# Weight conversion of a fused attention and feed-forward kernel: VectorE's bit steps with PSUM operands, one ScalarE copy more per block

## The chip, the cores and the metric

The kernel runs on one core of one Trainium2 chip. The metric is the device time of one execution in microseconds (us), as the median of several runs. Engines are named as in the profile: PE (TensorE, matrix products), DVE (VectorE), ACT (ScalarE), POOL (GpSimd) and SP (SyncE, which issues the DMAs here). They run side by side, each through its own queue in order, and wait for each other by semaphores. SBUF is the working memory; PSUM is the accumulation memory that PE writes, in 8 banks of 512 float32 columns on 128 partitions. DVE and ACT can read and write PSUM, POOL can't.

## The reference

```python
def _attn_ref(q, k, v):                      # q, k, v: (8, 8, 576, 64) float32
    scores = scale * np.matmul(q, k.transpose(0, 1, 3, 2))
    kth = np.partition(scores, -top_k, axis=-1)[..., -top_k:-top_k + 1]   # top_k = 32
    scores = np.where(scores >= kth, scores, -1000000000.0)
    attn = np.exp(scores - np.max(scores, axis=-1, keepdims=True))
    attn = attn / (np.sum(attn, axis=-1, keepdims=True) + 1e-09)
    return np.matmul(attn, v).astype(np.float32)

def _moe_ref(x, w_in, conv_w, w_out):        # x: (8, 576, 512); w_in: (512, 1024); w_out: (1024, 512)
    h = np.maximum(x @ w_in, 0.0)
    conv_out = ...                           # depthwise convolution of h with conv_w, 3 taps along the sequence
    gate = 1.0 / (1.0 + np.exp(-conv_out))
    return (h * gate @ w_out).astype(np.float32)
```

The attention output, with its heads side by side, is the input `x` of the gated feed-forward part. The weights `w_in`, `conv_w` and `w_out` arrive as float64. The chip has no float64 arithmetic, so the kernel turns each number into float32 by itself, from its two 32-bit words.

## The kernel before, in words

Attention goes by tiles of 128 query rows: 32 pairs of heads with 9 tiles each, 288 tiles (`NT`). A software pipeline handles them. `iteration(it)` issues, for each engine in an order written out by hand, one stage of each of some nine neighbouring tiles, and is called once per tile. In one iteration:

- PE transposes the weighted exponentials of an older tile (`transposes`, L306), computes scores of a pair of tiles into `s_ps` (`scores`, L214 to L222, every second iteration) and multiplies by V into a corner of the same PSUM tensor (`av`, L337 and L340).
- DVE finds the 32nd largest score: seven `MAX8` over chunks of a tile (`chunk_ops`, L235) interleaved with the merging of the candidates of the tile before (`cand_ops`, L255 and L257), one `MAX8` over a whole row (`below`, L283) and `select` (L287); then `weigh` (L293) masks the exponentials, which it reads from PSUM (`e_ps`), and sums them.
- ACT makes a sign mask (`sides`, L268), copies scores out of PSUM (`evacuate`, L228), copies transposed tiles (L311) and attention outputs (L348), and computes exponentials into `e_ps` (`expo`, L280). `e_ps` is a single buffer: `expo` of the next tile can start only when `weigh` has read it.
- POOL multiplies rows by the mask (`flip`, L273), and later does parts of the feed-forward convolution.

Feed-forward work (`Expand`, `Contract`) fills the rest of PE from 212 us on, when the first batch of attention outputs is there.

The change is in the conversion of the weights. 33 blocks (`weight_blocks`: one for `conv_w`, 16 for `w_in`, 16 for `w_out`, 256 numbers per partition each but for the first) go through a pipeline of their own, one block per iteration, so that all of it lies in the first 163 us. A block passes these steps:

- `load`: SP fetches the block's raw words into `raw`, up to 12 blocks ahead.
- `split` on DVE, in iteration k: L150 masks the exponent field out of the top 16-bit word of each number, L151 masks the top of the mantissa out of the upper 32-bit word. Both write to `scratch` in SBUF.
- `act` on ACT, at the end of the same iteration, after `expo`: L155 makes the power of two out of the exponent field (an `Exp`), L156 turns the mantissa's integer into float32, L157 does so with the lower 32-bit word (`rest`).
- `sign` on DVE, in iteration k+1: L161 puts the sign bit on the power; both of its tensor inputs and its output lie in SBUF.
- `pool` on POOL, in iteration k+2: L166, L170, L171 and L172 add the two mantissa parts, multiply by the signed power and split the product into two float32 parts for PE.

Where these steps stand on DVE is set by a loop at the end of the DVE part of `iteration`: `c_first` (the two split steps) after the first two chunk maxima, `c_last` (the sign) after the whole loop, just before `weigh`.

The PSUM bank `mc` belongs to the last product of the feed-forward part (`Contract`), whose first use comes after all blocks are converted.

Of the kernel before, what the change touches and what calls it, by code (L numbers as in the profile page):

```python
# [13 lines left out]
BF16 = mybir.dt.bfloat16  # L14
U16 = mybir.dt.uint16
U32 = mybir.dt.uint32
AF = mybir.ActivationFunctionType
ALU = mybir.AluOpType
# [32 lines left out]
WB = 256  # L51
# [12 lines left out]
def attend_and_feed(ctx: ExitStack, tc: tile.TileContext, q, k, v, weights, out, shared, finish=None):  # L64
    nc = tc.nc
# [13 lines left out]
    scale = 1.0 / float(D) ** 0.5  # L79
# [26 lines left out]
    offset = const.tile([P, 1], F32, name="offset")  # L106
# [11 lines left out]
    def bank(name):  # L118
        return ps.tile([P, BANK], F32, name=name, tag=name, bufs=1)
# [4 lines left out]
    scratch = []  # L124

    class Convert:
# [5 lines left out]
        def load(self):  # L132
            i = Convert.count
            Convert.count += 1
            if not scratch:
                scratch.append(moe.tile([P, 4 * SPB, WB], F32, name="scratch", tag="split"))
            self.at = i % SPB * 4
            tag = ("x_hi", "x_lo")[i % 2]
            self.raw = xp.tile([P, self.src.shape[-1], 2], U32, name="raw64", tag=tag)[0:self.n]
            nc.sync.dma_start(out=self.raw.rearrange("a c t -> a (c t)"), in_=self.src.bitcast(U32))  # L140
# [2 lines left out]
            return scratch[0][0:self.n, self.at + i, 0:self.raw.shape[1]]  # L143

        def split(self):
            exponent, self.mantissa, self.rest = (self.tmp(i) for i in range(3))
            n = exponent.shape[1]
            self.field, self.power = exponent.bitcast(U16)[:, 0:n], exponent.bitcast(BF16)[:, n:2 * n]
            self.top = self.raw.rearrange("a c t -> a (c t)").bitcast(U16).rearrange("a (c t) -> a c t", t=4)[:, :, 3]
            yield lambda: nc.vector.tensor_scalar(self.field, self.top, 0x7FF0, None, ALU.bitwise_and)  # L150
            yield lambda: nc.vector.tensor_scalar(self.mantissa.bitcast(U32), self.raw[:, :, 1], 0xFFFFF, 0x100000,  # L151
                                                  ALU.bitwise_and, ALU.bitwise_or)

        def act(self):
            nc.scalar.activation(out=self.power, in_=self.field, func=AF.Exp, scale=math.log(2.0) / 16, bias=offset)  # L155
            nc.scalar.activation(out=self.mantissa, in_=self.mantissa.bitcast(U32), func=AF.Copy, scale=2.0 ** -20)  # L156
            nc.scalar.activation(out=self.rest, in_=self.raw[:, :, 0], func=AF.Copy, scale=2.0 ** -52)  # L157

        def sign(self):
            power = self.power.bitcast(U16)  # L160
            yield lambda: nc.vector.scalar_tensor_tensor(out=power, in0=self.top, scalar=0x8000, in1=power,  # L161
                                                         op0=ALU.bitwise_and, op1=ALU.bitwise_or)

        def pool(self):
            x = self.mantissa
# [116 lines left out]
    def below(t):  # L282
        nc.vector.max(out=t.z[:, 0:8], in_=t.z[:, 10:S + 10])  # L283

    def select(t):
        hot = att.tile([P, 10], F32, name="hot", bufs=3)
        nc.vector.scalar_tensor_tensor(out=hot, in0=above, scalar=t.cnt, in1=t.z[:, 0:10],  # L287
                                       op0=ALU.is_equal, op1=ALU.mult, accum_out=kth[:, t.n:t.n + 1])
# [404 lines left out]
    def convert_dve():  # L693
        first, last = [], []
        while acted:
            c = acted.popleft()
            last.extend(c.sign())
            dved.append(c)
        if fetched:
            c = fetched.popleft()  # L700
            first.extend(c.split())
            cut.append(c)
        return first, last
# [10 lines left out]
    def iteration(it):  # L714
        nonlocal av_next, out_next, rec_next
        n = it + 3
# [14 lines left out]
        if n < NT:  # L731
# [3 lines left out]
            t = Box()  # L735
# [23 lines left out]
        c_first, c_last = convert_dve()  # L759
        for i in range(max(7, len(a_ops), len(b_ops))):  # L760
            if i < len(a_ops):
                a_ops[i]()
            for op in c_first[i:i + 1]:
                op()
            if tD is not None and not exact:
                if i == BELOW_AT:
                    below(tD)
                if i == BELOW_AT + 2:
                    select(tD)
            if i < len(b_ops):  # L770
                b_ops[i]()
        for op in c_last:
            op()
        while gates:
            gates.popleft().gate()
        recs, rec_next = rec_next, []
# [46 lines left out]
        while pool_tasks and state.pool > 0.2 and pool_tasks[0][0] <= it:  # L823
# [3 lines left out]
            _, c, fn = pool_tasks.popleft()  # L827
# [6 lines left out]
    with tc.manual_schedule(engines=engines) if engines else nullcontext():  # L834
        for pc in pcs[0:2]:
            fetch(pc)
        load_blocks(W_FIRST)
        for it in range(-3, NT + 6):
            iteration(it)
    if finish is not None:  # L840
        finish(corner(2, 1)[0:1])
    while expands or contracts or any(x.waiting for x in lanes) or pool_tasks or tanh_next or tanh_now or gates:
        it += 1
        iteration(it)
# [121 lines left out]
```

## Time and profile before

| | |
|---|---|
| median of 3 runs | 1152.47 us (1152.42 to 1154.94) |
| the profiled execution | 1155.28 us; its span, first to last instruction, 1153.4 us |
| busy, share of the span | PE 1035.3 us (90%), DVE 1064.5 (92%), ACT 996.5 (86%), POOL 895.6 (78%) |
| chain that ended last | DVE 45%, PE 42%, ACT 11% |
| TensorE clock | mean 0.963 of full; half speed for parts of 60 to 180 us, full for nearly all of the rest |

A busy time is the sum of an engine's instructions; the durations of neighbours overlap by some 0.08 us, since a following instruction starts before the former one has ended. "Idle before" is the time an engine stood still ahead of an instruction, with what ended it. The chain that ended last is followed back from the last instruction.

### The profile page before, as it was taken

How to read it: one execution, taken by the hardware profiler on the slowest of the kernel's cores; microseconds unless marked ns; L12 is line 12 of the kernel's file. 1: busy time of each engine (PE TensorE's matmuls, PEld its weight loads, DVE VectorE, ACT ScalarE, POOL GpSimd, SP SyncE). 2: the span in 40 equal slices, each digit the busy share in tenths (PEclk: the TensorE clock that was granted, in tenths of full speed). 3: DMA queues.
4: the chain of work that ended last, by engine and by line, in shares of the span. 5: the costliest groups of instructions: out<-in, count | busy, mean ns of one | idle time of the engine just before them, and what ended most of it. 6: DMA issues, size and time to landing. Idle time of an engine off the chain costs nothing.

```text
span 1153.4 us, 27267 instructions
## 1 busy us (share of the span) xinstructions
PE 1035.3 (90%) x7970; PEld 767.3 (67%) x7970; DVE 1064.5 (92%) x5834; ACT 996.5 (86%) x2343; POOL 895.6 (78%) x1078
## 2 busy tenths in 40 slices
PE   3665676788999999999999999999999999999997
PEld 1443444566767776777777767777777677777896
DVE  7999999999999999999999999999999999998651
ACT  5777868899999999999999999999999999998442
POOL 6788864688979888898978887987978897898300
PEclk9967659999999999999999999999999999999999
DMA  7221101111111111111111112121211011110001
GB/s 242 79 68 41 46 17 40 46 38 44 55 54 56 56 46 65 46 55 56 49 38 44 56 45 64 47 64 46 64 55 56 24 38 59 55 33 21 31 28 40
DMA packets 51694, 60.75 MB, mean 53 GB/s; under 512 B 9776, under 2 KB 30544, under 8 KB 51536
## 3 DMA queue, kind: packets, MB, share of 16 engines
q1 hardware_dynamic: 51536, 58.91, 16.0%
q8 instruction: 66, 1.08, 0.4%
q14 instruction: 92, 0.75, 0.2%
HBM read 49.31 MB, written 9.58 MB: 51 GB/s over the span
## 4 chain that ended last, share of the span: by engine, by line
DVE 45%; PE 42%; ACT 11%; issue 1%; DMA 0%; SPq 0%; POOL 0%; ACTq 0%; POOLq 0%
DVE cand L235 13%; DVE e L293 9%; PE mc L554 9%; PE me L404 8%; DVE z L283 7%; PE s_ps L337 6%; PE s_ps L219 5%; PE pt L306 5%; DVE cand L257 3%; ACT weights_ps L280 2%; DVE scratch L161 2%; DVE rows L255 2%; PE s_ps L222 2%; DVE hot L287 2%; PE weights_ps L554 2%; PE s_ps L214 2%
## 5 line engine op out<-in xcount | busy, mean ns | idle before, releaser
L273 POOL TENSOR_TENSOR z<-rows,side 128x579 f32<-128x579 f32 x288 | 347.4, 1206 | 143.0 <-ACT side L268 122.5
L235 DVE MAX8 cand<-rows 128x8 f32<-128x82 f32 (+1 forms) x2016 | 451.0, 238 | 0.0
L280 ACT ACTIVATE weights_ps<-rows,z 128x576 f32<-128x576 f32 x288 | 219.8, 763 | 42.4 <-DVE e L293 31.5
L293 DVE SCALAR_TENSOR_TENSOR e<-rows,kth,weights_ps 128x576 f32<-128x576 f32 x288 | 230.1, 799 | 0.3
L268 ACT ACTIVATE side<-rows 128x576 bf16<-128x576 f32 x288 | 224.2, 778 | 0.8 <-DVE rows L255 0.5
L404 PE MATMUL me<-x_hi,wi 128*128 128x322 f32 (+1 forms) x928 | 218.6, 308 | 1.2 <-ACT g L418 1.2
L283 DVE MAX8 z<-z 128x8 f32<-128x576 f32 x288 | 213.7, 742 | 0.0
L228 ACT COPY rows<-s_ps 128x576 f32<-128x576 f32 x288 | 183.0, 635 | 33.7 <-PE s_ps L340 20.3
L219 PE MATMUL s_ps<-k,q 64*128 64x512 f32 x512 | 155.1, 684 | 59.6 <-ACT xt L348 44.9
L306 PE MATMUL pt<-ident,e 128*128 128x128 f32 x1152 | 191.8, 292 | 8.9 <-DVE e L293 8.9
L337 PE MATMUL s_ps<-pT,vn 128*64 128x128 f32 (+1 forms) x2560 | 171.2, 279 | 17.7 <-ACT rows L228 17.7
L554 PE MATMUL mc<-wo,split 128*128 128x512 f32 x684 | 186.5, 406 | 0.0
L337 PEld LDWEIGHTS s_ps<-pT,vn 128*64 128x64 f32 x2560 | 134.3, 143 | 54.7 <-ACT rows L228 28.0
L306 PEld LDWEIGHTS pt<-ident,e 128*128 128x128 f32 x1152 | 135.3, 148 | 35.3 <-issue 20.1
L404 PEld LDWEIGHTS me<-x_hi,wi 128*128 128x128 f32 x928 | 157.1, 189 | 2.4 <-ACT g L418 2.1
L311 ACT COPY pT<-pt 128x512 f32<-128x512 f32 x256 | 152.0, 594 | 3.4 <-PE pt L306 3.2
L404 PE MATMUL me<-x_lo,wi 128*128 128x258 f32 (+1 forms) x464 | 138.5, 299 | 0.0
L554 PEld LDWEIGHTS mc<-wo,split 128*128 128x128 f32 x684 | 120.1, 189 | 19.6 <-issue 0.2
L437 POOL TENSOR_SCALAR t<-g,cr 128x256 f32<-128x256 f32 (+1 forms) x222 | 113.6, 512 | 0.0
L222 PEld LDWEIGHTS s_ps<-k,q 128*128 128x128 f32 x256 | 40.9, 201 | 105.6 <-issue 105.6
L255 DVE MAX8 rows<-cand 128x8 f32<-128x21 f32 x576 | 108.9, 189 | 0.2 <-issue 0.2
L219 PEld LDWEIGHTS s_ps<-k,q 64*128 64x128 f32 x512 | 40.6, 194 | 91.2 <-ACT xt L348 58.8
(121 smaller groups left out, 1865.6 us busy)
## 6 DMA issues: line engine op xcount, KB each, us to landing
k<-in_k_dram SPq DMA_DIRECT2D x32, 352.0 KB
q<-in_q_dram SPq DMA_DIRECT2D x32, 288.0 KB
vn<-in_v_main_dram SPq DMA_DIRECT2D x32, 256.0 KB
rb<-row SPq DMA_DIRECT2D x64, 128.0 KB
out_dram<-o SPq DMA_DIRECT2D x24, 256.0 KB
raw<-in_w_in_dram SPq DMA_DIRECT2D x16, 256.0 KB
raw<-in_w_out_dram SPq DMA_DIRECT2D x16, 256.0 KB
vt<-in_v_tail_dram SPq DMA_DIRECT2D x32, 64.0 KB
```

What stands on the lines that cost most here:

```text
L219: nc.tensor.matmul(s_ps[:, 2 * h * BANK:(2 * h + 1) * BANK], lhsT=qx[d, at], rhs=kx[d, h * TAIL:h * TAIL + MAIN], start=True, stop=True)
L228: nc.scalar.copy(out=x, in_=s_ps[:, at:at + S])
L235: yield lambda c=c, at=at, n=n: nc.vector.max(out=t.cand[:, c:8 * CHUNKS:CHUNKS], in_=t.x[:, at:at + n])
L268: nc.scalar.activation(out=t.side[:, 2:S + 2], in_=t.x, func=AF.Sign, scale=-OVER, bias=t.row[:, 7:8], accum_out=t.cnt)
L273: nc.gpsimd.tensor_tensor(t.z[:, 8:S + 11], t.row[:, 6:S + 9], t.side, ALU.mult)
L280: nc.scalar.activation(out=e_ps, in_=t.x, func=AF.Exp, scale=scale, bias=t.shift)
L283: nc.vector.max(out=t.z[:, 0:8], in_=t.z[:, 10:S + 10])
L293: nc.vector.scalar_tensor_tensor(out=t.e, in0=t.x, scalar=kth[:, t.n:t.n + 1], in1=e_ps, op0=ALU.is_ge, op1=ALU.mult, accum_out=t.pc.sums[ ...
L306: nc.tensor.transpose(tp[:, i * P:(i + 1) * P], t.e[:, o + i * P:o + (i + 1) * P], ident)
L337: nc.tensor.matmul(a[r, 0:w], lhsT=st.pc.vn[:, h, i], rhs=st.pT[:, h if st.i < NI else 1 - h, i, 0:w], start=(i == 0), stop=False)
L404: nc.tensor.matmul(mm[:, 0:w], lhsT=wt, rhs=xx, start=(n == 0), stop=(n == len(ops) - 1))
L554: nc.tensor.matmul(mm[0:m], lhsT=x[:, i], rhs=wo[:, e, f], start=start, stop=stop)
```

## The change

The bit steps work on whole 32-bit words, and their operands move to the PSUM bank `mc`: columns 0 to 255 are `field`, 256 to 511 `bits`. The two split steps read `raw` (SBUF) and write PSUM. ACT's `Exp` reads `field` from PSUM and writes bfloat16 to SBUF as before; a new ACT copy widens that to float32 into `field`; the mantissa step reads `bits` from PSUM. The sign step reads the power from PSUM and the raw word from SBUF and writes float32 to SBUF. The third difference is the place on DVE: for a block's turn in an iteration, the sign stands after the fifth chunk maximum (i = 4) and the two split steps after the sixth and seventh (i = 5 and 6).

```diff
             if not scratch:
                 scratch.append(moe.tile([P, 4 * SPB, WB], F32, name="scratch", tag="split"))
+                mc = bank("mc")
+                scratch.extend((mc[:, 0:WB], mc[:, WB:2 * WB]))
...
         def split(self):
-            exponent, self.mantissa, self.rest = (self.tmp(i) for i in range(3))
-            n = exponent.shape[1]
-            self.field, self.power = exponent.bitcast(U16)[:, 0:n], exponent.bitcast(BF16)[:, n:2 * n]
-            self.top = self.raw.rearrange("a c t -> a (c t)").bitcast(U16).rearrange("a (c t) -> a c t", t=4)[:, :, 3]
-            yield lambda: nc.vector.tensor_scalar(self.field, self.top, 0x7FF0, None, ALU.bitwise_and)
-            yield lambda: nc.vector.tensor_scalar(self.mantissa.bitcast(U32), self.raw[:, :, 1], 0xFFFFF, 0x100000,
+            self.power, self.mantissa, self.rest = (self.tmp(i) for i in range(3))
+            self.two = self.power.bitcast(BF16)[:, 0:self.power.shape[1]]
+            self.field, self.bits = (x[0:self.n, 0:self.raw.shape[1]] for x in scratch[1:])
+            self.top = self.raw[:, :, 1]
+            yield lambda: nc.vector.tensor_scalar(self.field.bitcast(U32), self.top, 0x7FF00000, None, ALU.bitwise_and)
+            yield lambda: nc.vector.tensor_scalar(self.bits.bitcast(U32), self.top, 0xFFFFF, 0x100000,
                                                   ALU.bitwise_and, ALU.bitwise_or)

         def act(self):
-            nc.scalar.activation(out=self.power, in_=self.field, func=AF.Exp, scale=math.log(2.0) / 16, bias=offset)
-            nc.scalar.activation(out=self.mantissa, in_=self.mantissa.bitcast(U32), func=AF.Copy, scale=2.0 ** -20)
+            nc.scalar.activation(out=self.two, in_=self.field.bitcast(U32), func=AF.Exp, scale=math.log(2.0) / 2 ** 20,
+                                 bias=offset)
+            nc.scalar.copy(out=self.field, in_=self.two)
+            nc.scalar.activation(out=self.mantissa, in_=self.bits.bitcast(U32), func=AF.Copy, scale=2.0 ** -20)
             nc.scalar.activation(out=self.rest, in_=self.raw[:, :, 0], func=AF.Copy, scale=2.0 ** -52)

         def sign(self):
-            power = self.power.bitcast(U16)
-            yield lambda: nc.vector.scalar_tensor_tensor(out=power, in0=self.top, scalar=0x8000, in1=power,
-                                                         op0=ALU.bitwise_and, op1=ALU.bitwise_or)
+            yield lambda: nc.vector.scalar_tensor_tensor(out=self.power.bitcast(U32), in0=self.top, scalar=0x80000000,
+                                                         in1=self.field.bitcast(U32), op0=ALU.bitwise_and,
+                                                         op1=ALU.bitwise_or)
...
             if i < len(a_ops):
                 a_ops[i]()
-            for op in c_first[i:i + 1]:
+            for op in (c_last + c_first)[i - 4:i - 3] if i > 3 else ():
                 op()
...
-        for op in c_last:
-            op()
         while gates:
```

Line numbers of the changed kernel are 2 to 4 higher: the split steps are L152 and L153, the sign L164; on ACT the `Exp` is L157, the new copy L159, the mantissa L160, `rest` L161; the chunk maxima are L239, `select` L291, `weigh` L297, `expo` L284.

DVE's queue in one iteration of the conversion, before, from the first chunk maximum (a name in brackets is the engine or DMA queue whose semaphore the instruction waits for; `raw_161` and `raw_159` are two neighbouring blocks):

```order
L235 MAX cand<-rows 128x8
L150 TENSOR_SCALAR scratch<-raw_161 128x256 [waits DMAHW7_49]
L255 MAX rows<-cand 128x8 [waits DVE_49]
L235 MAX cand<-rows 128x8
L151 TENSOR_SCALAR scratch<-raw_161 128x256 [waits Pool_49]
L257 MATCH_REPLACE cand<-rows,cand 128x21 [waits DVE_49]
```

and the end of that iteration:

```order
L287 SCALAR_TENSOR_TENSOR hot,kth<-weights_ps,cnt,z 128x10 [waits Activation_49]
L255 MAX rows<-cand 128x8 [waits DVE_49]
L235 MAX cand<-rows 128x8 x2
L161 SCALAR_TENSOR_TENSOR scratch<-raw_159,scratch 128x256 [waits Activation_49]
L293 SCALAR_TENSOR_TENSOR e_492,sums<-rows,kth,weights_ps 128x576 [waits DVE_49,PE_49]
```

The same end of an iteration now:

```order
L261 MATCH_REPLACE cand<-second,cand 128x35 [waits DVE_49]
L239 MAX cand<-rows 128x8
L164 SCALAR_TENSOR_TENSOR scratch<-raw_159,mc 128x256 [waits Activation_49]
L291 SCALAR_TENSOR_TENSOR hot,kth<-weights_ps,cnt,z 128x10
L259 MAX rows<-cand 128x8 [waits DVE_49]
L239 MAX cand<-rows 128x8
L152 TENSOR_SCALAR mc<-raw_161 128x256 [waits DMAHW6_49,DVE_49]
L239 MAX cand<-rows 128x8
L153 TENSOR_SCALAR mc<-raw_161 128x256 [waits DVE_49]
L297 SCALAR_TENSOR_TENSOR e_401,sums<-rows,kth,weights_ps 128x576
```

The split steps went from the head of the iteration to its end, and the sign from the end to the place ahead of `select` (L291); the first five chunk maxima and the merging between them now stand ahead of the sign with no bit step among them.

ACT's queue from `expo` to the end of its part of an iteration, before:

```order
L280 ACTIVATE weights_ps<-rows,z 128x576 [waits DVE_49,Pool_49]
L155 ACTIVATE scratch<-scratch,offset 128x256
L156 ACTIVATE scratch<-scratch 128x256
L157 ACTIVATE scratch<-raw_275 128x256 [waits DMAHW1_49]
L268 ACTIVATE side_113,cnt<-rows 128x576 [waits Activation_49]
```

and now:

```order
L284 ACTIVATE weights_ps<-rows,z 128x576 [waits DVE_49,Pool_49]
L157 ACTIVATE scratch<-mc,offset 128x256
L159 CAST mc<-scratch 128x256 [waits Activation_49]
L160 ACTIVATE scratch<-mc 128x256 [waits Activation_49]
L161 ACTIVATE scratch<-raw_282 128x256 [waits DMAHW1_49]
L272 ACTIVATE side_109,cnt<-rows 128x576
```

One instruction more stands there, and two waits of ACT for itself: the copy for the `Exp`, and the mantissa step for the copy, which writes the same bank. In the built program the sign's wait for ACT before is one for L155, and now one for L160, the last of the three steps that use the bank.

## Rows read from the trace of the kernel before

**Rows 1.** Busy time by stretch: us, engines busy (x instructions), PEclk, DMA share, GB/s

```profile
11.40:25.57 14.17, 7.54 (x18) 2.51 (x14) 14.17 (x66) 11.39 (x27) 12.35 (x18) 1.00 0.72 257
25.57:159.38 133.81, 81.81 (x470) 51.59 (x470) 133.67 (x596) 97.84 (x240) 109.97 (x141) 0.76 0.17 53
```

**Rows 2.** Groups by line and form, DVE, 25.57 to 159.38 us: busy us, mean ns

```profile
L161 DVE SCALAR_TENSOR_TENSOR scratch<-raw,scratch 128x256 uint16<-128x256 uint16 x28 | 28.1, 1004 | 0.0
L293 DVE SCALAR_TENSOR_TENSOR e<-rows,kth,weights_ps 128x576 f32<-128x576 f32 x27 | 21.6, 801 | 0.0
...
L150 DVE TENSOR_SCALAR scratch<-raw 128x256 uint16<-128x256 uint16 x26 | 15.1, 579 | 0.0
...
L151 DVE TENSOR_SCALAR scratch<-raw 128x256 uint32<-128x256 uint32 x26 | 11.0, 423 | 0.0
```

**Rows 3.** Timeline, DVE, first blocks, POOL at rest: start us, us

```profile
8.51 0.29 DVE L150 TENSOR_SCALAR scratch<-raw 128x256 uint16<-128x256 uint16 x1 [1.21 <-DMA raw<-in_w_in_dram]
...
11.39 0.42 DVE L161 SCALAR_TENSOR_TENSOR scratch<-raw,scratch 128x256 uint16<-128x256 uint16 x1
```

**Rows 4.** Timeline, DVE and POOL, 24 to 27 us

```profile
24.17 1.20 POOL L273 TENSOR_TENSOR z<-rows,side 128x579 f32<-128x579 f32 x1
24.24 1.41 DVE L161 SCALAR_TENSOR_TENSOR scratch<-raw,scratch 128x256 uint16<-128x256 uint16 x1
...
25.33 0.90 POOL L166 TENSOR_TENSOR scratch<-scratch 128x256 f32<-128x256 f32 x1
...
25.73 0.65 DVE L150 TENSOR_SCALAR scratch<-raw 128x256 uint16<-128x256 uint16 x1
```

**Rows 5.** Timeline, DVE, one iteration of the conversion

```profile
129.14 0.80 DVE L293 SCALAR_TENSOR_TENSOR e<-rows,kth,weights_ps 128x576 f32<-128x576 f32 x1
...
129.87 0.24 DVE L235 MAX8 cand<-rows 128x8 f32<-128x83 f32 x1
130.03 0.67 DVE L150 TENSOR_SCALAR scratch<-raw 128x256 uint16<-128x256 uint16 x1
...
130.86 0.33 DVE L151 TENSOR_SCALAR scratch<-raw 128x256 uint32<-128x256 uint32 x1
...
132.62 0.20 DVE L287 SCALAR_TENSOR_TENSOR hot<-weights_ps,cnt,z 128x10 f32<-128x10 f32 x1
...
133.17 1.26 DVE L161 SCALAR_TENSOR_TENSOR scratch<-raw,scratch 128x256 uint16<-128x256 uint16 x1
134.36 0.80 DVE L293 SCALAR_TENSOR_TENSOR e<-rows,kth,weights_ps 128x576 f32<-128x576 f32 x1
```

**Rows 6.** Timeline, ACT, the same iteration

```profile
128.65 0.64 ACT L228 COPY rows<-s_ps 128x576 f32<-128x576 f32 x1 [1.16 <-PE s_ps L340]
...
130.04 0.75 ACT L280 ACTIVATE weights_ps<-rows,z 128x576 f32<-128x576 f32 x1
130.72 0.19 ACT L263 COPY edge<-rows 128x14 f32<-128x14 f32 x1
130.81 0.50 ACT L155 ACTIVATE scratch<-scratch,offset 128x256 bf16<-128x256 uint16 x1
131.22 0.40 ACT L156 ACTIVATE scratch<-scratch 128x256 f32<-128x256 uint32 x1
...
135.26 0.75 ACT L280 ACTIVATE weights_ps<-rows,z 128x576 f32<-128x576 f32 x1 [1.39 <-DVE e L293]
```

**Rows 7.** Groups by line and form, DVE, 300 to 1050 us: a PSUM input

```profile
L473 DVE SCALAR_TENSOR_TENSOR g<-weights_ps,g 128x256 f32<-128x256 f32 x42 | 17.1, 407 | 0.0
```

**Rows 8.** Timeline: a DVE wait for DVE, and one for ACT

```profile
10.11 0.20 DVE L191 RECIPROCAL cr<-cr 128x8 f32<-128x8 f32 x1
10.35 0.44 DVE L192 TENSOR_TENSOR cr<-cr,cw 128x8 f32<-128x8 f32 x1
...
168.81 0.76 ACT L280 ACTIVATE weights_ps<-rows,z 128x576 f32<-128x576 f32 x1
...
169.60 0.23 DVE L287 SCALAR_TENSOR_TENSOR hot<-weights_ps,cnt,z 128x10 f32<-128x10 f32 x1 [1.51 <-ACT weights_ps L280]
```

## The prediction

> **What bounds the kernel now.** I read the page's share of busy time first, which says only that all engines are loaded, and then the busy time by stretch. From 25.57 to 159.38 us, where nearly all of the conversion lies, DVE is busy 133.67 of 133.81 us, ACT 97.84, and PE runs at a mean granted clock of 0.76 [rows 1]. So in this stretch DVE sets the pace and every other engine has time to spare. `weigh` runs 27 times in it [rows 2], which makes 27 iterations of 133.81 / 27 = 4.96 us. All 33 blocks are converted in the first 163 us; nothing in the remaining thousand is touched by the change, and the order of work there is fixed by the iteration's number. What the stretch gains, the end should gain.
>
> The groups by line give the share of the three bit steps: the sign L161 takes 1004 ns, the field L150 579, the mantissa bits L151 423 on average [rows 2]. A following instruction starts some 0.08 us before the end of the former: `weigh` starts at 129.14, lasts 0.80, and the next begins at 129.87 [rows 5]. Less 0.08 each, the three hold DVE for 0.92 + 0.50 + 0.34 = 1.76 us of the 4.96. The rest of an iteration is 4.96 - 1.76 = 3.20.
>
> These steps are not slow by themselves. The reader is to compare the first blocks, where POOL rests, with a later one: the field takes 0.29 there and the sign 0.42 [rows 3]; while POOL runs its flip the sign takes 1.41, and the field beside POOL's addition 0.65 [rows 4]. The other long DVE instructions don't spread like this: `weigh`, which reads one tensor from SBUF and one from PSUM, has a mean of 801 ns in the stretch [rows 2] and 0.80 in each of the two places of one iteration [rows 5]. So it is steps with both inputs, or input and output, in SBUF that are held up by POOL. That is what the change takes away.
>
> **The change, part by part.** The three steps on DVE. The nearest row for the new sign is the gate L473: the same operation at 128x256, one input in PSUM, one in SBUF, output in SBUF, with POOL at work beside it: 407 ns [rows 7]. Less 0.08 that is 0.33. For the two split steps, which read SBUF and write PSUM, the trace has no row of that size. Bounds: 0.29, the field with POOL at rest [rows 3], and 0.65, beside POOL [rows 4]. I take 0.41, as for L473, since that is the row with an operand in PSUM; it lies nearer the lower bound. The Trainium skill, "VectorE: DVE Perf Modes", section "Why PSUM operands drop a tier", says that an operand in PSUM takes the mode with two results per cycle from a float32 operation with one input, which speaks against the change: each split step would lose that half. By it the steps cost what I took; without it they would cost 0.29, and 26 iterations would gain 2 x 0.12 x 26 = 6.2 us more. No run so far shows it. Three steps of 0.33 are 1.0 us in place of 1.76: DVE's own work falls to 3.20 + 1.0 = 4.20 us per iteration.
>
> The wait of the sign. Before, the sign stood at the end of the iteration, more than an iteration's half behind the last ACT step that it needed. Now it stands earlier, and it waits for three ACT steps instead of one. Counted from the first chunk maximum (129.87): `expo` starts at 130.04, when `weigh` has freed its buffer, and holds ACT to 130.72, so the `Exp` can start at 0.85 (the `edge` copy of 0.09 comes only once in seven iterations) [rows 6]. Then `Exp` 0.50, copy 0.40, mantissa 0.40, by L155 and L156 [rows 6]; the copy has no row before, and L156 is the same size on the same engine. Each of the two new self-waits I put at 0.04, as DVE's for itself (10.11 + 0.20 = 10.31 to 10.35), and the hand-over to DVE at 0.03 (168.81 + 0.76 = 169.57 to 169.60) [rows 8]. Sum: 0.85 + 0.50 + 0.04 + 0.40 + 0.04 + 0.40 + 0.03 = 2.26.
>
> DVE reaches the sign after what stood before `select`, without the two split steps: 132.62 - 129.87 - 0.59 - 0.25 = 1.91 [rows 5]. So it waits 0.35 us for ACT in each iteration, with `select`, two chunk maxima, both split steps and `weigh` queued behind it; and `weigh` is what releases the next `expo`. That closes a loop: 2.26 up to the sign, then sign 0.33, `select` to the last maxima 133.17 - 132.62 = 0.55, split 2 x 0.33, `weigh` 0.73, together 2.27 [rows 5]. The loop takes 4.53 us; DVE's work of 4.20 fits in it.
>
> ACT. The copy and the lost overlap add 0.3 + 2 x 0.1 + 2 x 0.04 = 0.6 us to 97.84 / 27 = 3.6 us of busy time per iteration [rows 1]: about 4.2 of 4.53. Before, the cover was ACT's wait for `weigh`, 1.39 us at 135.26 [rows 6]; about 0.3 of it is left. At the seam between two pairs of heads, once in nine iterations, `evacuate` waits 1.16 for PE [rows 6]. That cost nothing before; now some 0.9 of it comes through, 0.10 per iteration. So 4.63 in the mean.
>
> POOL. Its multiplication reads float32 for the power where it read bfloat16, and its first addition no longer meets the sign on DVE. Both are under 0.15 us, and POOL is busy 109.97 of 133.81 [rows 1]: nothing. SP and the DMAs stay as they are: the blocks are up to 12 ahead. The `mc` bank is free until the first `Contract`, which comes after all blocks: nothing.
>
> Sum: (4.96 - 4.63) x 26 iterations with all three steps = 8.6 us. Before 25.57 three more iterations hold the same steps on a DVE that never rests [rows 1]; there the steps save 0.76 and the wait takes back 0.35, 1.2 us for three. Together 9.8, in round numbers 10. On the profiled execution that is 1155.28 - 10 = 1145.3; the median of the runs lies 2.8 below it: **1142 us**. Its own range is 1136 (split steps at 0.29, self-waits hidden) to 1147 (ACT's steps 0.1 longer each, most of the seam's wait coming through).
>
> **The rivals.** *The full saving*: the sign finds ACT done, and all of DVE's 0.76 comes through: 29 x 0.76 = 22 us, 1130. For it: the chain is late by 0.35 only, and ACT may be quicker with PSUM. If the sign waited for the copy alone, the chain would be 1.82, under the 1.91. Against it: the wait goes by the bank, and the third step is in it. On this the Trainium skill, "PSUM — Partial Sum Buffer", section "PSUM bank collisions raise a hardware error", says that two engines on the same bank at once, even both reading, in other columns too, collide, and that semaphores must guard the bank. By that rule the sign has to stay behind the mantissa step and the time is 1142, not 1130; no run so far shows a collision.
>
> *The steps don't get shorter*: if the split steps stay as long as beside POOL, because reading `raw` from SBUF is enough to be held up, they hold DVE 0.84 instead of 0.66 on average and up to 1.1 in the worst iteration; the loop is then 4.7 to 5.0, with the seam 4.8 to 5.1, and the time 1148 to 1153, say 1151: no change. Against it: the steady `weigh`.
>
> *A new wait that costs more than the old steps*: ACT becomes the bound. The place is the chain `Exp`, copy, mantissa, all three behind `expo` and ahead of the sign. It decides from the point where the chain is 4.96 - 4.63 = 0.33 us longer than my 2.26; each further 0.1 us costs 2.6 us. If a self-wait of ACT holds it 0.25 instead of 0.04, and the copy takes 0.5, the chain is 2.78, the iteration 5.15, and the kernel 26 x 0.19 = 5 us slower: 1157. For it: no row shows ACT waiting for itself, and at the lower clock PE may hand over later than at the seam of [rows 6]. Against it: DVE's self-wait is 0.04.
>
> *The gain is partly given back*: the clock of PE is 0.76 in the stretch [rows 1], and the iterations that follow may lean on PE; then half of the 10 us is lost, 1147.
>
> **How the numbers follow.** Two measurements of this kernel can be told apart from about 0.3%, 3.5 us. The forecast has 0.55, the full saving 0.20, no shorter steps 0.11, the ACT bound 0.07, the part given back 0.07. Faster by over 0.3% (below 1149.0): 0.55 + 0.20 + 0.06 = 0.81. Within 0.3%: 0.11 + 0.01 = 0.12. Slower: 0.07. The range must reach the full saving and, with its split steps at 0.29, a little below it: 1128. Upward it takes in most of the case without change: 1151. Outside lie the ACT bound and a third of that case, and a few hundredths below.
>
> **What would show it.** In the profile after: the sign near 410 ns with no spread, the split steps between 290 and 420; DVE idle ahead of the sign, released by the mantissa step on ACT, some 0.35 us times 26; ACT's wait for `weigh` down to some tenths; the last conversion at about 153 us instead of 163, and the same time from there to the end. The prediction is wrong if the split steps still take over 500 ns, if DVE shows no idle time ahead of the sign (then 1130), or if the iterations of the stretch take 5 us with ACT busy throughout.

## The result and the profile after

The changed kernel took 1141.9 us (median of 4 runs, 1141.32 to 1143.56), the kernel before 1153.51 beside it; the ratio is 0.9901, 95% interval [0.9884, 0.9918]. The forecast of 1142.0 and its range held. The profiled execution took 1141.93 us, its span 1140.1.

Busy time by stretch, of the kernel before from the end of its conversion stretch on, and of the changed kernel in its conversion stretch and behind it (columns as in [rows 1]):

```profile
159.38:1153.00 993.62, 942.30 (x7476) 711.69 (x7476) 913.29 (x5146) 882.88 (x2067) 771.20 (x905) 0.99 0.15 47
```

```profile
25.00:146.40 121.40, 75.03 (x476) 46.27 (x476) 114.53 (x596) 111.49 (x274) 106.85 (x140) 0.79 0.19 58
146.40:1140.00 993.60, 941.04 (x7476) 711.34 (x7476) 913.74 (x5146) 883.58 (x2068) 772.55 (x908) 0.99 0.15 47
```

From the first start of `weigh` to the 27th, 26 iterations, it took 129.01 us before (29.64 to 158.65, 4.96 each) and 117.62 after (28.61 to 146.23, 4.52 each): 11.4 us there, 1.0 ahead of it. From the 27th start of `weigh` to the end of the span it took 994.8 us before and 993.9 after, so 0.9 more is gained there. (The rows on the rest of the kernel agree to 0.02 us because they do not begin at the same point of the work: the first begins 0.7 us behind that start, the second 0.2.) So 12.4 of the 13.3 us between the two spans lie in the conversion. And DVE, which never rested in this stretch [rows 1], now stands still for some 7 of 121 us.

Groups of DVE by line and form, 25 to 146.4 us, in place of [rows 2]:

```profile
L297 DVE SCALAR_TENSOR_TENSOR e<-rows,kth,weights_ps 128x576 f32<-128x576 f32 x27 | 21.6, 801 | 0.0
...
L164 DVE SCALAR_TENSOR_TENSOR scratch<-raw,mc 128x256 uint32<-128x256 uint32 x27 | 11.4, 422 | 6.7 <-ACT scratch L160 6.7
L153 DVE TENSOR_SCALAR mc<-raw 128x256 uint32<-128x256 uint32 x27 | 11.2, 414 | 0.0
L152 DVE TENSOR_SCALAR mc<-raw 128x256 uint32<-128x256 uint32 x26 | 10.8, 414 | 0.0
```

The three steps take 422, 414 and 414 ns, where they took 1004, 423 and 579. `weigh` takes 801 as before. Behind the sign's last bar stands the new wait: 6.7 us, for ACT's mantissa step L160.

One iteration, DVE and then ACT, in place of [rows 5, 6]:

```profile
111.64 0.25 DVE L239 MAX8 cand<-rows 128x8 f32<-128x83 f32 x1
...
113.81 0.42 DVE L164 SCALAR_TENSOR_TENSOR scratch<-raw,mc 128x256 uint32<-128x256 uint32 x1 [0.19 <-ACT scratch L160]
...
114.57 0.41 DVE L152 TENSOR_SCALAR mc<-raw 128x256 uint32<-128x256 uint32 x1
...
115.04 0.42 DVE L153 TENSOR_SCALAR mc<-raw 128x256 uint32<-128x256 uint32 x1
115.36 0.80 DVE L297 SCALAR_TENSOR_TENSOR e<-rows,kth,weights_ps 128x576 f32<-128x576 f32 x1
```

```profile
111.82 0.74 ACT L284 ACTIVATE weights_ps<-rows,z 128x576 f32<-128x576 f32 x1 [0.23 <-DVE e L297]
112.50 0.45 ACT L157 ACTIVATE scratch<-mc,offset 128x256 bf16<-128x256 uint32 x1
112.98 0.38 ACT L159 CAST mc<-scratch 128x256 f32<-128x256 bf16 x1
113.39 0.38 ACT L160 ACTIVATE scratch<-mc 128x256 f32<-128x256 uint32 x1
```

The reader can follow the loop that the prediction drew: `weigh` ends, `expo` starts at 111.82, then `Exp`, copy, mantissa; at 113.77 the last of them ends and at 113.81 the sign starts, 2.17 us after the first chunk maximum. From there to the next first chunk maximum, which follows `weigh` at 116.09, it is 2.28. A plain iteration, the commonest one, takes 4.45 us.

### The profile page after: what moved, and what is told of

It reads as the page before. It is cut to its first block, busy times and chain, and to the rows that moved or that the text cites. A ratio compares the mean times of both kernels' runs of the same rounds, so it can differ in the third digit from the quotient of the medians.

```text
span 1140.1 us, 27318 instructions
## 1 busy us (share of the span) xinstructions
PE 1024.5 (90%) x7970; PEld 760.6 (67%) x7970; DVE 1043.7 (92%) x5834; ACT 1009.7 (89%) x2376; POOL 891.5 (78%) x1078
## 4 chain that ended last, share of the span: by engine, by line
PE 41%; DVE 39%; ACT 16%; issue 2%; DMA 0%; POOL 0%; SPq 0%; ACTq 0%; POOLq 0%
DVE cand L239 12%; DVE e L297 10%; PE mc L558 9%; PE me L408 8%; DVE z L287 6%; PE s_ps L341 5%; PE pt L310 5%; PE s_ps L223 5%; ACT weights_ps L284 4%; DVE cand L261 3%; DVE hot L291 2%; DVE rows L259 2%; PE weights_ps L558 2%; PE s_ps L226 2%; PE s_ps L218 2%
## 5 line engine op out<-in xcount | busy, mean ns | idle before, releaser
L239 DVE MAX8 cand<-rows 128x8 f32<-128x82 f32 (+1 forms) x2016 | 456.9, 240 | 0.1
L284 ACT ACTIVATE weights_ps<-rows,z 128x576 f32<-128x576 f32 x288 | 220.0, 764 | 15.9 <-DVE e L297 9.1
L297 DVE SCALAR_TENSOR_TENSOR e<-rows,kth,weights_ps 128x576 f32<-128x576 f32 x288 | 230.6, 801 | 0.2
L223 PE MATMUL s_ps<-k,q 64*128 64x512 f32 x512 | 152.6, 674 | 63.7 <-ACT xt L352 45.7
L310 PE MATMUL pt<-ident,e 128*128 128x128 f32 x1152 | 189.5, 289 | 1.9 <-DVE e L297 1.6
L341 PE MATMUL s_ps<-pT,vn 128*64 128x128 f32 (+1 forms) x2560 | 168.4, 276 | 16.6 <-ACT rows L232 16.6
L341 PEld LDWEIGHTS s_ps<-pT,vn 128*64 128x64 f32 x2560 | 131.9, 141 | 53.0 <-ACT rows L232 26.7
L310 PEld LDWEIGHTS pt<-ident,e 128*128 128x128 f32 x1152 | 133.0, 146 | 27.6 <-issue 15.8
```

What stands on the lines that cost most here:

```text
L223: nc.tensor.matmul(s_ps[:, 2 * h * BANK:(2 * h + 1) * BANK], lhsT=qx[d, at], rhs=kx[d, h * TAIL:h * TAIL + MAIN], start=True, stop=True)
L239: yield lambda c=c, at=at, n=n: nc.vector.max(out=t.cand[:, c:8 * CHUNKS:CHUNKS], in_=t.x[:, at:at + n])
L284: nc.scalar.activation(out=e_ps, in_=t.x, func=AF.Exp, scale=scale, bias=t.shift)
L297: nc.vector.scalar_tensor_tensor(out=t.e, in0=t.x, scalar=kth[:, t.n:t.n + 1], in1=e_ps, op0=ALU.is_ge, op1=ALU.mult, accum_out=t.pc.sums[ ...
L310: nc.tensor.transpose(tp[:, i * P:(i + 1) * P], t.e[:, o + i * P:o + (i + 1) * P], ident)
L341: nc.tensor.matmul(a[r, 0:w], lhsT=st.pc.vn[:, h, i], rhs=st.pT[:, h if st.i < NI else 1 - h, i, 0:w], start=(i == 0), stop=False)
```

## The experiments

Theory A, as the prediction had it: steps with all operands in SBUF are held up by POOL; operands in PSUM take that away, at the price of slower split steps, the ACT copy and the sign's wait. Theory B: the new places on DVE count, not the operands. Theory C: the wait for ACT costs nothing that could be had back.

| run | operands of the steps | place on DVE | median us | ratio to before | weigh to weigh, us |
|---|---|---|---|---|---|
| before | SBUF | old | 1153.51 | 1 | 4.96 |
| the change | PSUM | new | 1141.9 | 0.9901 [0.9884, 0.9918] | 4.52 |
| e5, the change again | PSUM | new | 1140.77 | 0.9866 [0.9824, 0.9907] | 4.53 |
| e1 | SBUF | new | 1134.91 | 0.9821 [0.9779, 0.9862] | 4.32 |
| e9, e1 again | SBUF | new | 1133.66 | 0.9818 [0.9788, 0.9847] | 4.33 |
| e6 | sign PSUM, splits SBUF | old | 1143.58 | 0.9895 [0.9848, 0.9942] | 4.62 |
| e7 | splits PSUM, sign SBUF | old | 1175.0 | 1.0159 [1.0116, 1.0201] | 5.84 |
| e8 | splits PSUM, sign SBUF | new | 1135.69 | 0.9831 [0.979, 0.9872] | 4.37 |
| e2 | PSUM | after the loop | 1139.09 | 0.9852 [0.981, 0.9893] | 4.41 |
| e3 | PSUM | two places earlier | 1178.93 | 1.018, one run | 5.76 |
| e4 | PSUM, mantissa ahead of copy | new | 1135.63 | 0.982 [0.9778, 0.9863] | 4.38 |
| e12 | as e4 | spread out | 1133.69 | 0.9805 [0.9766, 0.9843] | 4.20 |
| e10 | SBUF, POOL's order turned | new | 1146.28 | 0.992 [0.9896, 0.9943] | 4.76 |
| e11 | PSUM, POOL's order turned | new | 1145.55 | 0.9921 [0.9892, 0.9951] | 4.58 |

The last column is the mean over the same 26 iterations, from the starts of `weigh`. Runs e1 to e4, e5 to e8 and e9 to e12 each shared a chip; before took 1157.76, 1155.5 and 1154.76 us there, and the ratios are to these. Run e5 is the change once more: 14.7 us under the kernel before on its chip, where the first measurement gave 11.6.

**e1, the place alone.** The kernel before with only the loop of the change:

```diff
-            for op in c_first[i:i + 1]:
+            for op in (c_last + c_first)[i - 4:i - 3] if i > 3 else ():
...
-        for op in c_last:
-            op()
```

> The kernel before with nothing changed but the places of the three steps on VectorE (sign, field, bits after the fifth, sixth and seventh chunk maximum); operands stay in SBUF. Theory A (the gain comes from operands that POOL does not hold up): the steps keep their old means (1.0, 0.58, 0.42 us), the iteration stays at 4.96 us, the time at 1153 +- 4 us. Theory B (the gain comes from the place): 1142 us.

Both theories missed: the move alone gains more than the whole change. Groups of DVE, 25 to 146.4 us:

```profile
L161 DVE SCALAR_TENSOR_TENSOR scratch<-raw,scratch 128x256 uint16<-128x256 uint16 x27 | 14.5, 535 | 0.0
L151 DVE TENSOR_SCALAR scratch<-raw 128x256 uint32<-128x256 uint32 x26 | 12.4, 477 | 0.0
L150 DVE TENSOR_SCALAR scratch<-raw 128x256 uint16<-128x256 uint16 x26 | 8.5, 326 | 0.0
```

All operands lie in SBUF, and yet the sign's mean is 535 ns instead of 1004. What differs is what POOL does at the start of each step. Timeline of POOL in the iteration of [rows 5], before:

```profile
129.88 0.67 POOL L170 TENSOR_TENSOR scratch<-scratch 128x256 f32<-128x256 f32 x1
130.64 0.40 POOL L171 TENSOR_SCALAR wo<-scratch 128x256 fp32r<-128x256 f32 x1
...
132.95 1.20 POOL L273 TENSOR_TENSOR z<-rows,side 128x579 f32<-128x579 f32 x1 [1.09 <-ACT side L268]
```

The sign starts at 133.17 [rows 5], and the flip ends at 134.15. The sign's 1.26 us are 134.15 - 133.17 - 0.14 = 0.84, and then the 0.42 that it takes alone [rows 3], together 1.26. In the same way the field at 130.03: 130.55 - 130.03 - 0.14 = 0.38, and 0.28 alone (0.29 in [rows 3]): 0.66, for 0.67 in the row; the bits at 130.86: 0.04 + 0.28 = 0.32, for 0.33. All 96 steps of 256 columns of the kernel before fit this within 0.02 us: a step waits until 0.14 before the recorded end of the POOL instruction that runs when it starts, one-input instructions (L171) among them, and then takes its time alone; with less than 0.14 us left it starts at once. 24 of the 32 signs start during a flip. Timeline of e1, DVE and then POOL:

```profile
111.25 0.41 DVE L161 SCALAR_TENSOR_TENSOR scratch<-raw,scratch 128x256 uint16<-128x256 uint16 x1
...
112.00 0.35 DVE L150 TENSOR_SCALAR scratch<-raw 128x256 uint16<-128x256 uint16 x1
...
112.42 0.41 DVE L151 TENSOR_SCALAR scratch<-raw 128x256 uint32<-128x256 uint32 x1
```

```profile
110.50 0.72 POOL L166 TENSOR_TENSOR scratch<-scratch 128x256 f32<-128x256 f32 x1
111.30 0.89 POOL L170 TENSOR_TENSOR scratch<-scratch 128x256 f32<-128x256 f32 x1
112.28 0.41 POOL L171 TENSOR_SCALAR wo<-scratch 128x256 fp32r<-128x256 f32 x1
```

The sign starts in the gap between two POOL instructions and runs in 0.41; it is POOL that waits, 0.89 for its multiplication instead of 0.67. 21 of the 32 signs start while POOL stands still, 20 of them within 0.06 us of its next instruction. The Trainium skill, "SBUF — State Buffer", section "Who interferes with whom", says that the two engines share a pair of ports, that the instruction which comes first has it to its end, and that the other stands still. The traces agree, for both sides.

So theory A's mechanism stood, with a new part: what the steps lose to POOL depends on where they fall in POOL's cycle, and a move on DVE changes that as much as a change of operands.

**e10 and e11, the test of that: POOL's order turned.** In both, the last two of POOL's four conversion steps go behind the flip (e10 from e1, e11 from the changed kernel); nothing on DVE or ACT moves:

```diff
-                nc.gpsimd.tensor_scalar(self.dst, x, 1.0, 0.0, ALU.mult, ALU.add)
-                nc.gpsimd.tensor_tensor(self.low, x, f32(self.dst), ALU.subtract)
+                halved.append(self)
...
         if not flipped:
             flip(tC)
+        while halved:
+            halved.pop().pool_end()
```

> The kernel before with the new places alone once more (all operands in SBUF), beside the next three on one chip. Theory A and B: 1135 (1132 to 1138), period of weigh 4.32 us.

> As the run before, and POOL's order turned: the last two of its four conversion steps come after the flip instead of ahead of it, so that the bit steps meet other POOL instructions. Nothing else is moved. Theory A (the gain of the places comes from where the steps fall in POOL's cycle): the three steps' means no longer add up to 1.34 us but to 1.5 or more, each still POOL's rest less 0.14 plus its time alone; 1137 to 1152, I take 1143. Theory B (the place on DVE is what counts, whatever POOL does): 1135, the steps as in the run before.

> The changed kernel (operands in PSUM) with POOL's order turned in the same way. Theory A: the steps don't see POOL, 0.41 to 0.42 each; period 4.52, 1141 (1138 to 1144). If operands in PSUM do not shield the steps: they spread as in the run before, and the time moves with it by more than 3 us.

Groups of DVE, 25 to 146.4 us, of e10 and then of e11:

```profile
L151 DVE TENSOR_SCALAR scratch<-raw 128x256 uint32<-128x256 uint32 x25 | 21.1, 845 | 0.0
...
L161 DVE SCALAR_TENSOR_TENSOR scratch<-raw,scratch 128x256 uint16<-128x256 uint16 x26 | 14.7, 567 | 0.0
L150 DVE TENSOR_SCALAR scratch<-raw 128x256 uint16<-128x256 uint16 x26 | 9.6, 371 | 0.0
```

```profile
L153 DVE TENSOR_SCALAR mc<-raw 128x256 uint32<-128x256 uint32 x27 | 11.2, 414 | 0.0
L164 DVE SCALAR_TENSOR_TENSOR scratch<-raw,mc 128x256 uint32<-128x256 uint32 x26 | 10.9, 421 | 7.9 <-ACT scratch L160 7.8
L152 DVE TENSOR_SCALAR mc<-raw 128x256 uint32<-128x256 uint32 x26 | 10.7, 413 | 0.0
```

With operands in SBUF the steps now add up to 1.78 us, the bits step to 845 ns, because it falls on the flip; the time rises by 12.6 us over e9, on the same chip, with DVE's order unchanged. Theory B falls. With operands in PSUM the three durations don't move by more than a nanosecond. Its iteration is 0.05 longer, of which 0.04 is the sign's wait; the median lies 1.6 above the range given, and 4 to 5 us over those of the change, which were not taken beside it. The trace is of the fastest of its four executions (1142.67 us), which is only 0.7 longer than the change's 1141.93; the 26 iterations take 1.4 more in it. The steps did not spread, but why the other three executions took 1145 to 1147 stays open.

**e6 and e7, the operands alone, at the old places.** In e6 only the sign's power goes through PSUM:

```diff
+            nc.scalar.copy(out=scratch[1][0:self.n, 0:self.raw.shape[1]], in_=self.power)
...
+            self.power = self.tmp(3)
+            yield lambda: nc.vector.scalar_tensor_tensor(out=self.power.bitcast(U32), in0=self.raw[:, :, 1],
+                                                         scalar=0x80000000, in1=wide.bitcast(U32),
+                                                         op0=ALU.bitwise_and, op1=ALU.bitwise_or)
```

> All three steps at their old places; only the sign's power goes through PSUM (with the new ACT copy), the splits stay as before. Theory A: the sign falls from 1.00 to 0.41 us, each of them, with no wait on ACT (it stands at the end of the iteration); period 4.96 - 0.59 = 4.37 us, 26 x 0.59 = 15 us and 1 to 2 us early: 1136 (1130 to 1144, as the splits meet POOL at another point of its cycle). Theory B (place): nothing is moved, one ACT copy more: 1152 to 1158.

Groups of DVE, 25 to 146.4 us:

```profile
L152 DVE TENSOR_SCALAR scratch<-raw 128x256 uint32<-128x256 uint32 x26 | 17.1, 656 | 0.0
L151 DVE TENSOR_SCALAR scratch<-raw 128x256 uint16<-128x256 uint16 x25 | 15.6, 623 | 0.0
L164 DVE SCALAR_TENSOR_TENSOR scratch<-raw,mc 128x256 uint32<-128x256 uint32 x26 | 10.3, 397 | 0.0
```

The sign fell to 397 ns, as A said, without a wait, and 26 of 26 stayed there. But the splits, still in SBUF, rose from 579 and 423 to 623 and 656 ns: a shorter sign lets them start at another point of POOL's cycle, and 63 of these 64 steps fit the same rule. Of 0.59 us per iteration, 0.35 came through. Theory B (1152 to 1158) missed, A's range held at its edge.

In e7 only the splits write PSUM, as L152 and L153 of the change, in the old places:

> All three steps at their old places; only the two split steps write PSUM, in 32-bit words, the sign stays as before in SBUF. Theory A: field and bits 0.41 each with no spread (before 0.58 and 0.42 in the mean): period 4.96 - 0.18 = 4.78, about 1147; the sign, still in SBUF, 0.4 to 1.4 as it meets POOL, which makes it 1140 to 1153. Rival D (the read of raw in SBUF is enough to be held up): split steps spread up to 0.65 and more, mean over 0.5: 1152 to 1158.

A miss by 28 us. Groups of DVE, and its waits (total, times, longest), 25 to 146.4 us:

```profile
L153 DVE TENSOR_SCALAR mc<-raw 128x256 uint32<-128x256 uint32 x21 | 9.0, 427 | 28.0 <-ACT scratch L161 28.0
L155 DVE TENSOR_SCALAR mc<-raw 128x256 uint32<-128x256 uint32 x21 | 8.7, 413 | 0.0
```

```profile
DVE mc L153 <- ACT scratch L161: 28.0, 20, 1.8
```

The split steps did not spread, so rival D falls too. What I had not seen is that the bank holds one block: at the head of the iteration the next block's field must wait until ACT has read the block before, and ACT reads it only behind `expo`, which waits for `weigh`. With a single bank, the old places cost this. (The same waits list puts 28.9 us of `expo`, 14 times, down to POOL's multiplication. In all 14 `expo` starts 0.10 us after the recorded end of `weigh`, the same distance as in the kernel before and in the change, so it is `weigh` that releases it; POOL's instruction happens to end 0.01 us ahead of `expo`.)

**e2, e3, e4: the wait for ACT.** All three are the changed kernel with one thing moved: e2 the steps behind the whole loop, e3 two places earlier, e4 ACT's copy behind its mantissa step:

```diff
+            nc.scalar.activation(out=self.mantissa, in_=self.bits.bitcast(U32), func=AF.Copy, scale=2.0 ** -20)
             nc.scalar.copy(out=self.field, in_=self.two)
-            nc.scalar.activation(out=self.mantissa, in_=self.bits.bitcast(U32), func=AF.Copy, scale=2.0 ** -20)
```

> The changed kernel with all three steps moved behind the loop, just ahead of weigh. Theory A (the iteration of 4.45 us is the loop weigh, expo, three ACT steps, sign, weigh; VectorE has 0.26 us of idle time in it): VectorE reaches the sign 0.55 us later, at 2.46 us after the first maximum, when ACT has been done since 2.17; no wait is left, the iteration falls to VectorE's work of 4.20 or to ACT's of some 4.25, 26 x 0.2 to 0.25 = 5 to 6.5 us less: 1136 to 1137 us. Theory C (only the sum of VectorE's work decides): the same as the changed kernel, 1142 us.

> The changed kernel with the three steps two places earlier (after the third, fourth and fifth chunk maximum), the same instructions on every engine. Theory A: ACT's chain ends where it did, so 1.2 us of VectorE's work moves from ahead of the sign to behind it; the iteration grows from 4.45 to about 5.6 us, the sign waits some 1.4 us, 26 x 1.2 = 31 us more: about 1173 us, slower than the kernel before. Theory C: 1142 us.

> The changed kernel with ACT's mantissa step ahead of the new copy (Exp, mantissa, copy): the copy then finds the Exp finished, and the mantissa step overlaps the Exp's end. Theory A: the chain to the sign is 0.19 us shorter (2.17 to about 1.98), the iteration 4.27 us, 26 x 0.19 = 5 us less: 1137 us. Theory C: 1142 us.

e3: the sign waits 27.5 us, 19 times in the stretch, the iteration takes 5.76 us for the 5.6 that A said, and the kernel, in its one execution, is slower than before. Waits of DVE, 25 to 146.4 us (total, times, longest):

```profile
DVE scratch L164 <- ACT scratch L160: 27.5, 19, 1.6
```

e4: the idle time ahead of the sign falls to 2.9 us in the stretch, 1.8 of it for ACT, and the plain iteration from 4.45 to 4.31, where A said 4.27. e2: no wait for ACT is left, but the steps are neighbours. Timeline of DVE:

```profile
102.46 0.40 DVE L164 SCALAR_TENSOR_TENSOR scratch<-raw,mc 128x256 uint32<-128x256 uint32 x1
102.90 0.43 DVE L152 TENSOR_SCALAR mc<-raw 128x256 uint32<-128x256 uint32 x1
103.36 0.43 DVE L153 TENSOR_SCALAR mc<-raw 128x256 uint32<-128x256 uint32 x1
103.70 0.80 DVE L297 SCALAR_TENSOR_TENSOR e<-rows,kth,weights_ps 128x576 f32<-128x576 f32 x1
```

Each starts only after the end of the one before: 0.44 and 0.46 from start to start instead of 0.33, since in the built program each waits for DVE's own access to the bank. That is some 0.24 us per iteration, and e2's median lies half way between A and C; e3 and e4 speak for A.

**e8, the sign in SBUF at the new place.** The changed kernel, but the copy writes `tmp(3)` in SBUF and the sign reads it there:

> The changed kernel, but the ACT copy writes SBUF and the sign reads it there; places and split steps as in the change. Theory A: the sign does not wait for the mantissa step any more (ACT's chain is 1.77 us, DVE arrives after 1.9), but it is held up whenever POOL runs an instruction at its start: 0.41 to 1.4 us with spread, each by POOL's rest less 0.14 plus 0.41; period 4.2 to 4.7, 1132 to 1147, I take 1139. Theory B (place): 1135, as with all operands in SBUF at the new places, and no step held up.

Groups of DVE, 25 to 146.4 us:

```profile
L164 DVE SCALAR_TENSOR_TENSOR scratch<-raw,scratch 128x256 uint32<-128x256 uint32 x27 | 15.2, 562 | 0.8 <-ACT scratch L159 0.8
```

The wait is gone but for 0.8 us, and the sign is held up again: 562 ns in the mean, 0.40 to 0.96, each of the 32 by the same rule within 0.02. Here that costs less (0.14 us per sign) than the wait did (0.26).

**e12, both costs away.** e4 with the sign one place later, the field behind the last chunk maximum, the bits behind `weigh`:

```diff
-            for op in (c_last + c_first)[i - 4:i - 3] if i > 3 else ():
+            for op in (c_last + c_first)[i - 5:i - 4] if i > 4 else ():
...
             weigh(tD)
+        for op in (c_last + c_first)[2:]:
+            op()
```

> The changed kernel with ACT's mantissa step ahead of its copy, the sign one place later (after the sixth chunk maximum), the field after the seventh and the mantissa bits behind weigh, so that no two of the steps in the bank stand next to each other. Theory A: no wait of DVE for ACT in the plain iterations, no wait in the bank, so that only the work is left: 3.20 + 3 x 0.33 = 4.2 us plain, 4.35 in the mean; 26 x 0.61 + 1.5 = 17 us less than before: 1136 (1133 to 1138). Theory C (steps with PSUM operands cost more than their durations show): 1140 or more.

Weigh to weigh is 4.15 plain and 4.20 in the mean, the best of all runs: the prediction's 3.20 + 1.0, with neither a wait nor a spread in the plain iterations. Its median is 8 us under the change's and equals e9's, on the same chip. It ends the 26 iterations at 135.64 us, 4.4 ahead of e9, and gives that back at once. Busy time by stretch, e12 and then e9:

```profile
160.00:185.00 25.00, 18.31 (x139) 11.57 (x139) 23.20 (x141) 19.67 (x47) 9.69 (x8) 0.80 0.17 53
```

```profile
160.00:185.00 25.00, 16.81 (x164) 11.04 (x164) 24.93 (x149) 21.80 (x52) 10.97 (x10) 1.00 0.17 53
```

In e12 PE's granted clock is 0.80 in the mean there, so at its lower level of 1.2 GHz for a part, in e9 it is 1.00, 2.4 GHz; from the 27th `weigh` to the 50th e12 takes 80.25 us and e9 74.94. That the clock causes this was not tested. The runs of e12 spread from 1129.16 to 1136.02; the shortest has the highest mean granted clock (0.980), the two longest the lowest (0.972), which fits but does not settle it.

## Why the prediction was right

**The steps.** Predicted 0.41 each, without spread; measured 414, 414 and 422. The split steps did get slower than they are alone in SBUF: 414 ns for 0.28 us. The Trainium skill, "VectorE: DVE Perf Modes", section "Why PSUM operands drop a tier", says that an operand in PSUM takes such a step's faster mode away, and the traces agree. That the read of `raw` alone could hold them up (the rival without shorter steps) is excluded by the change itself, where 44 of the 64 split steps of 256 columns start while a POOL instruction runs and all take 410 to 428 ns, and by e11.

**The wait.** Predicted 2.26 us from the first chunk maximum to the sign, measured 2.17: `Exp` 0.45 for 0.50, the copies 0.38 for 0.40, the self-waits 0.03 for 0.04. DVE arrived at 1.98 instead of 1.91. So the wait is 0.19 in a plain iteration and 6.7 / 26 = 0.26 in the mean, for 0.35. The second half of the loop is 2.28 for 2.27.

**ACT.** Its wait for `weigh` is 5.6 us, 20 times, 0.28 each, where the prediction left about 0.3. An iteration is 4.52 us in the mean, for 4.63.

**The sum.** 26 x (4.96 - 4.52) = 11.4 and 1.0 early, for 8.6 and 1.2: 12.4 for 9.8; the last conversion ends at 151.9 us instead of 163.2, where the prediction said about 153. Between the profiled executions the difference is 13.35 us. That the median came out within 0.1 of the forecast is partly luck: the medians lie 11.6 apart, because the profiled execution of before lay 1.8 to 2.8 above its medians, and that of after on its own.

**The rivals.** The full saving needed a sign that finds ACT done; e8 and e12 made that, with plain iterations of 4.16 and 4.15, for the 4.20 of the prediction, and beside the kernel before on their own chips they are 19.8 and 21.1 us shorter, close to the 22 of this rival. In the traces e12 is 23.0 us ahead of the kernel before at the 27th `weigh`, and 2.3 of that are lost behind it. So the full saving was there to be had, but not with the sign waiting for ACT. The wait that costs more than the old steps is real at other places: e3 and e7. Nothing was given back in the change: from the 27th `weigh` on 993.9 us for 994.8.

**The step that failed.** "So it is steps with both inputs, or input and output, in SBUF that are held up by POOL. That is what the change takes away." The first sentence holds for these three steps and is too wide for DVE as a whole: the `MAX8` over a row (`below`, L283) has its input and its output in SBUF too, ran beside POOL all 27 times, and took 734 to 743 ns:

```profile
L283 DVE MAX8 z<-z 128x8 f32<-128x576 f32 x27 | 19.9, 736 | 0.0
```

The second sentence is half of it: the prediction took 0.92 + 0.50 + 0.34 us as a property of the operands and costed the move only as the cause of the sign's wait. The move alone, e1, takes away more than the change does, since it puts the sign in a gap of POOL; the PSUM operands then add a wait, and cost 6 to 7 us against it (the 27th `weigh` starts at 146.23 us, in e1 at 139.14, in e9 at 140.00). What they buy is that the steps' durations no longer hang on POOL's order: turned, that costs the SBUF version 12.6 us, and the PSUM version 4 to 5 in the median, for which its steps, unchanged, are not the cause.

## What to carry to other kernels

When a DVE instruction's duration spreads while POOL works, lay its start against POOL's timeline before changing its operands: if it waits out the POOL instruction that runs, moving it in its queue can be worth as much as moving its data. Operands in PSUM made these steps immune (393 to 443 ns over all runs), but a single bank shared by two engines makes a chain: keep the steps that touch it off each other's heels, and put the consumer behind the last producer's arrival. Judge each step where it will stand, for shortening one shifts all the others against POOL.

## What the runs showed of the hardware

- A bit step with all its operands in SBUF stands still until 0.14 us before the recorded end of the running POOL instruction, with two inputs or one. In before all 96 such steps fit within 0.02 us, in e10 93. In the other 3 both engines start within 0.02 us of each other, DVE runs at its own speed and POOL waits, its flip taking 1.35 us instead of 1.20. Timeline of e10, DVE and then POOL:

```profile
50.85 0.27 DVE L151 TENSOR_SCALAR scratch<-raw 128x256 uint32<-128x256 uint32 x1
```

```profile
50.84 1.35 POOL L276 TENSOR_TENSOR z<-rows,side 128x579 f32<-128x579 f32 x1 [1.12 <-ACT side L271]
```

- Here the two engines, which hold each other up, settled in a good rhythm or a bad one. In e1 and e9 the first eight iterations take 4.10 to 4.11 us each; in before they take 4.95 to 5.21, with the same instructions in another order on DVE, and 24 of 32 signs on the flip.
- The copy from SBUF into PSUM, a size that the trace before did not show, took 376 ns on ACT; the same copy into SBUF took 405 (e8). The mantissa step was faster with its input in PSUM, 383 ns where it took 402, and so was the `Exp`, 459 where it took 496, though its input changed from 16 to 32 bits as well.
